# Another layout for the tokens of k and v: five on each of 112 partitions and the last 16 apart, in place of four on each of 128 and separate rest rows

## The chip, the cores and the metric

The kernel runs on one core of a Trainium2 chip. The metric is the device time of one execution in microseconds (us). A run counts as fast or slow by its state, and verdicts use fast runs alone. A ratio is the mean time of one kernel's fast runs over the mean of the other's fast runs of the same rounds, so it is not quite the ratio of the medians quoted beside it. Intervals are 95%.

## The reference, cut to what matters

```python
# batch 8, heads 8, sequence 576, head dimension 64
phi = lambda x: np.where(x > 0, x, np.exp(x) - 1.0) + 1.0
q_p, k_p = phi(q), phi(k)
kv  = np.einsum('bhsd,bhse->bhde', k_p, v)        # summed over the 576 tokens
z   = np.sum(k_p, axis=2)
num = np.einsum('bhsd,bhde->bhse', q_p, kv)
den = np.einsum('bhsd,bhd->bhs', q_p, z)[..., None] + 1e-06
x   = (num / den).transpose(0, 2, 1, 3).reshape(4608, 512)
out = gelu_tanh(x @ w_in) @ w_out                 # 512 -> 2048 -> 512
```

576 tokens are four and a half times 128. The sum over tokens does not depend on their order, so k and v may be laid out over the partitions in any way, as long as both are laid out alike.

## The kernel before

TensorE is kept busy with the feed-forward layers of one batch (a "stage") while the other engines prepare the attention of later batches. Most loads and all transposes by DMA share one queue, issued by SyncE (SP); the rest rows of later batches are issued by GpSimd (POOL). Of each tensor of a batch, 512 tokens are loaded as four tokens on each of 128 partitions. The other 64 tokens, the "rest rows", of two batches share one tile (64 partitions each).

```python
pld  = tile_pool(name="pld", bufs=6)     # staging tiles of all loads
psm  = tile_pool(name="psm", bufs=2)     # transposed rest rows of q, qtr
px   = tile_pool(name="px", bufs=5)      # result tiles
...
def load_main(src, b, name, eng, parts=1):          # P = 128, C = 4, MAIN = 512
    t = pld.tile([P, H, C * D], FP32, name=name, tag="ld")
    ... out=t[:, i*hs:(i+1)*hs, :],
        in_=src[b, i*hs:(i+1)*hs, 0:MAIN, :].rearrange("h (p c) d -> p h (c d)", c=C)

def load_rest_half(src, t, m, s, eng):              # REST = 64
    eng.dma_start(out=t[REST*s : REST*(s+1)],
                  in_=src[2*m + s, :, MAIN:S, :].rearrange("h p d -> p h d"))
...
vps = [const.tile([P, H, C, E], BF16, name=f"vp{i}") for i in range(2)]
vrs = [[const.tile([P, H, E], BF16, name=f"vr{i}{s}") for s in range(2)] for i in range(2)]
...
def kv_mm(b, i, kv_ps, at_i=None):
    for c in range(C):
        nc.tensor.matmul(dst, lhsT=kp[:, c, P*i : P*(i+1)], rhs=vps[b%2][:, 2*i:2*i+2, c, :], ...)
    nc.tensor.matmul(dst, lhsT=kr[:, 0, P*i : P*(i+1)], rhs=vrs[(b//2)%2][b%2][:, 2*i:2*i+2, :], ...)
```

The cuts are marked with "...". The weights w_in and w_out go through the same staging tiles: four pieces each, loaded as f32, cast to bf16 by GpSimd, one half of the last w_out piece by ScalarE.

## Time and profile before

| | before |
|---|---|
| time, median of 3 runs | 296.39 us (295.96 to 296.93) |
| profiled span, granted TensorE clock | 293.6 us, 1.000 |
| TensorE busy / idle in the span | 285.3 / 8.3 us |
| second w_out piece landed (from the trace) | 36.63 us |
| stages 0 to 8 (from one batch's first gelu to the next one's, the last to the end) | 31.8, 30.8, 30.0, 30.1, 30.2, 29.7, 30.2, 27.6, 30.3 us |

The first gelu starts at 22.9 us, and the stages fill the rest. The last stage but one is short because less work lies beside the feed-forward layers there. The prediction below shows the lines of the page and the timeline.

### The profile page before, as it was taken

Reading aid. Unit: us, or ns where it says so; the run is one execution under the profiler, and the core shown is the slowest. Engines: PE = TensorE matmul, PEld = TensorE weight load, DVE = VectorE, ACT = ScalarE, POOL = GpSimd, SP = SyncE. Lnnn points to the kernel's source line nnn. Section 1 sums busy time; section 2 is a strip of 40 time slices with the busy share of each in tenths; the row PEclk is TensorE's granted clock in tenths of the full one; section 3 lists DMA queues with packets and bytes.
Section 4 is the critical chain, followed back from the end, with each engine's and each line's share of the span. In section 5 each row is a group of like instructions: output and inputs, shape, how many; then the busy total and the mean of one; then the engine's idle time right before and its main releaser. Section 6 shows DMA issues by size and latency. Waiting matters only on the chain.

```text
span 293.6 us, 4284 instructions
## 1 busy us (share of the span) xinstructions
PE 285.3 (97%) x1701; PEld 149.8 (51%) x1730; DVE 114.4 (39%) x189; ACT 159.2 (54%) x221; POOL 37.1 (13%) x56
## 2 busy tenths in 40 slices
PE   8999999999999999999999999999999999999995
PEld 6885446644565545544454445544554444444443
DVE  3660576245486684356125652543241000000002
ACT  4657963679955772567255935682560176017400
POOL 8057077400005200000000000000000000000000
PEclk9999999999999999999999999999999999999999
DMA  7999999994599969949913895304241110021032
GB/s 238 328 405 394 370 363 384 318 363 143 151 345 243 185 203 341 190 59 288 307 65 71 245 312 126 71 2 139 75 62 30 71 74 0 4 94 47 0 71 71
DMA packets 63731, 53.23 MB, mean 181 GB/s; under 512 B 31712, under 2 KB 56544, under 8 KB 63712
## 3 DMA queue, kind: packets, MB, share of 16 engines
q1 hardware_dynamic: 60288, 41.82, 50.7%
q10 hardware_dynamic: 2464, 8.52, 7.4%
q0 software_dynamic: 960, 2.62, 3.4%
q8 instruction: 13, 0.21, 0.3%
q14 instruction: 6, 0.05, 0.1%
HBM read 36.70 MB, written 9.44 MB: 157 GB/s over the span
## 4 chain that ended last, share of the span: by engine, by line
PE 84%; DMA 11%; DVE 2%; POOL 1%; issue 1%; SPq 0%; ACT 0%; DVEq 0%
PE o_ps L734 39%; PE h_ps L306 37%; DMA w_st<-in_moe_w_out_dram 8%; DMA q_x<-in_q_dram 3%; PE n_ps L258 3%; PE kv_ps L224 2%; PE o_ps L703 1%; POOL w_out_sb L153 1%; PE t_ps L281 1%; DVE kvbd L247 1%; PE kv_ps L231 1%; SPq L67 0%; ACT q_e L165 0%; PE t_ps L252 0%; DVE xt L388 0%
## 5 line engine op out<-in xcount | busy, mean ns | idle before, releaser
L734 PE MATMUL o_ps<-w_out_sb,g 128*128 128x512 bf16 x547 | 123.7, 379 | 1.3 <-POOL w_out_sb L153 0.4
L306 PE MATMUL h_ps<-xt,w_in_sb 128*128 128x512 bf16 (+2 forms) x566 | 118.9, 353 | 0.8
L691 ACT ACTIVATE g<-h_ps 128x512 bf16<-128x512 f32 x144 | 84.4, 598 | 49.9 <-PE h_ps L306 49.0
L734 PEld LDWEIGHTS <-g 128*128 128x128 bf16 x560 | 54.1, 98 | 63.5 <-issue 1.1
L306 PEld LDWEIGHTS <-w_in_sb 128*128 128x128 bf16 x644 | 58.2, 98 | 54.4 <-issue 0.5
L749 ACT COPY o_sb<-o_ps 128x512 f32<-128x512 f32 x18 | 10.5, 585 | 57.7 <-PE o_ps L734 53.1
L747 DVE COPY o_sb<-o_ps 128x512 f32<-128x512 f32 x17 | 11.7, 689 | 64.5 <-PE o_ps L734 57.2
L270 DVE TENSOR_TENSOR x<-n_ps,r 128x512 bf16<-128x512 f32 x36 | 24.9, 692 | 1.2
L247 DVE CAST kvbd<-kv_ps 64x260 bf16<-64x260 f32 (+1 forms) x16 | 6.5, 409 | 39.2 <-PE kv_ps L231 39.1
L165 ACT ACTIVATE q_e<-q_x 128x2048 bf16<-128x2048 f32 (+1 forms) x10 | 15.5, 1557 | 3.1 <-DMA q_x<-in_q_dram 3.1
L165 ACT ACTIVATE k_e<-k_x 128x2048 bf16<-128x2048 f32 (+1 forms) x9 | 15.5, 1719 | 2.8 <-DMA k_x<-in_k_dram 2.7
L268 DVE RECIPROCAL r<-n_ps 128x8 f32<-128x8 f32 x36 | 7.4, 206 | 24.0 <-PE n_ps L258 24.0
L182 DVE TENSOR_TENSOR k_p<-k_p,k_e 128x2048 bf16<-128x2048 bf16 (+1 forms) x9 | 10.7, 1193 | 13.5 <-ACT k_e L165 13.3
L333 PE MATMUL w_ps<-warm 128*128 128x252 bf16 x94 | 14.0, 315 | 1.1 <-DVE warm L124 1.1
L176 DVE TENSOR_SCALAR q_p<-q_x 128x2048 bf16<-128x2048 f32 (+1 forms) x10 | 10.7, 1068 | 8.8 <-DMA q_x<-in_q_dram 8.8
L306 PE MATMUL h_ps<-xt_rest,w_in_sb 128*128 128x512 bf16 x62 | 13.9, 379 | 0.1
L258 PEld LDWEIGHTS <-qt 128*128 128x128 bf16 x128 | 9.7, 98 | 7.9 <-issue 1.0
L208 DVE CAST vp<-v_x 128x2048 bf16<-128x2048 f32 (+1 forms) x9 | 9.4, 1045 | 9.9 <-DMA v_x<-in_v_dram 9.9
L258 PE MATMUL n_ps<-kvbd,qt 128*128 128x130 bf16 x128 | 12.7, 221 | 0.6 <-ACT kvbd L247 0.2
L224 PEld LDWEIGHTS <-k_p 128*128 128x128 bf16 x128 | 9.6, 96 | 6.1 <-DVE vp L208 0.7
L224 PE MATMUL kv_ps<-vp,k_p 128*128 128x130 bf16 x128 | 11.9, 220 | 0.4 <-DVE vp L208 0.4
L333 PEld LDWEIGHTS <-warm 128*128 128x128 bf16 x94 | 10.4, 114 | 3.2 <-DVE warm L124 1.1
(52 smaller groups left out, 141.3 us busy)
## 6 DMA issues: line engine op xcount, KB each, us to landing
out_dram<-o_sb ACTq DMA_DIRECT2D x16, 512.0 KB, 4.9
k_x<-in_k_dram SPq DMA_DIRECT2D x7, 1024.0 KB, 5.9
v_x<-in_v_dram SPq DMA_DIRECT2D x7, 1024.0 KB, 12.4
q_x<-in_q_dram SPq DMA_DIRECT2D x6, 1024.0 KB, 9.0
w_st<-in_moe_w_in_dram SPq DMA_DIRECT2D x4, 1024.0 KB, 10.1
w_st<-in_moe_w_out_dram SPq DMA_DIRECT2D x4, 1024.0 KB, 11.3
q_x<-in_q_dram SPq DMA_DIRECT2D x4, 512.0 KB, 9.9
k_x<-in_k_dram SPq DMA_DIRECT2D x2, 512.0 KB, 4.1
```

What stands on the lines that cost most here:

```text
L165: nc.scalar.activation(e[:, :, hs, :].rearrange("p c h d -> p h c d"), by_chunk(x[:, hs]), AF.Exp)
L176: nc.vector.tensor_scalar(xp[:, :, hs, :].rearrange("p c h d -> p h c d"), by_chunk(x[:, hs]), 1.0, 1.0, op0=ALU.add, op1=ALU.max,)
L182: nc.vector.tensor_tensor(xp[:, :, hs, :], xp[:, :, hs, :], e[:, :, hs, :], op=ALU.min)
L224: nc.tensor.matmul(dst, lhsT=kp[:, c, P * i : P * (i + 1)], rhs=vps[b % 2][:, 2 * i : 2 * i + 2, c, :], start=(c == 0), stop=False,)
L258: nc.tensor.matmul(n_ps[rows, i // 2, 2 * E * (i % 2) : 2 * E * (i % 2) + 2 * E], lhsT=qt_c[:, i, rows], rhs=kvbd[:, i, :], skip_group_che ...
L270: nc.vector.tensor_tensor(x, n_v[:, :, :, 0:D], r[:, :, :, None].to_broadcast([P, 2, 4, D]), op=ALU.mult,)
L306: nc.tensor.matmul(h_ps[:, tok], lhsT=w_in_sb[:, c, P * m : P * (m + 1)], rhs=xt[:, c, tok], start=(c == 0), stop=(c == KM - 1), skip_grou ...
L333: nc.tensor.matmul(w_ps[:, 0:252], lhsT=warm[:, 0:P], rhs=warm)
L691: nc.scalar.activation(gs[j][:, i, :], ps, AF.Gelu_apprx_tanh)
L734: nc.tensor.matmul(o_pss[t], lhsT=g[:, m, P * t : P * (t + 1)], rhs=w_out_sb[:, m, :], start=(m == 0), stop=(m == MM - 1),)
L747: nc.vector.tensor_copy(dst, o_ps)
L749: nc.scalar.copy(dst, o_ps)
```

## The change

The intent is to be rid of the rest rows of k and v: small loads that reach only half of the partitions, with maps and casts of their own. Tokens 0 to 559 now lie five each on 112 partitions. The last 16 lie on the other 16 partitions, in the fifth chunk only. The fifth matmul sums over all 128 partitions, the first four over 112. Two buffer counts are lowered in the same diff.

```diff
+    CK = 5
+    PK = 112
-    psm = ctx.enter_context(tc.tile_pool(name="psm", bufs=2))
-    px = ctx.enter_context(tc.tile_pool(name="px", bufs=5))
+    psm = ctx.enter_context(tc.tile_pool(name="psm", bufs=1))
+    px = ctx.enter_context(tc.tile_pool(name="px", bufs=4))
...
+    def load_kv(src, b, name, parts=1, eng=nc.sync):
+        t = staged(name, LD).rearrange("p (h x) -> p h x", h=H)
         eng.dma_start(
+            out=t[PK:P, :, C * D :], in_=src[b, :, PK * CK : S, :].rearrange("h p d -> p h d")
         )
+        hs = H // parts
+        for i in range(parts):
+            s = slice(i * hs, (i + 1) * hs)
+            nc.sync.dma_start(
+                out=t[0:PK, s],
+                in_=src[b, s, 0 : PK * CK, :].rearrange("h (p c) d -> p h (c d)", c=CK),
+            )
+        return t
...
-    vps = [const.tile([P, H, C, E], BF16, name=f"vp{i}") for i in range(2)]
-    vrs = [
-        [const.tile([P, H, E], BF16, name=f"vr{i}{s}") for s in range(2)]
-        for i in range(2)
-    ]
+    vps = [const.tile([P, H, CK, E], BF16, name=f"vp{i}") for i in range(2)]
...
+    def pieces(n):
+        if n < CK:
+            return ((slice(0, P), slice(0, n)),)
+        return (slice(0, PK), slice(0, C)), (slice(0, P), slice(C, CK))
...
-        for c in range(C):
+        for c in range(CK):
+            r = slice(0, P if c == C else PK)
             nc.tensor.matmul(
                 dst,
-                lhsT=kp[:, c, P * i : P * (i + 1)],
-                rhs=vps[b % 2][:, 2 * i : 2 * i + 2, c, :],
+                lhsT=kp[r, c, P * i : P * (i + 1)],
+                rhs=vps[b % 2][r, 2 * i : 2 * i + 2, c, :],
```

The exponential, the two maps and the cast of v each loop over `pieces`. Rest rows stay for q alone. In batch 0 the small transfers of the last 16 tokens are issued by ScalarE (`eng=nc.scalar`), all others by SyncE.

## The prediction

> **What bounds the kernel now.** I read the busy table first, then the chain that ended last and the groups, to see whether the engines that the change touches set the time.
>
> ```profile
> PE 285.3 (97%) x1701; PEld 149.8 (51%) x1730; DVE 114.4 (39%) x189; ACT 159.2 (54%) x221; POOL 37.1 (13%) x56
> ...
> PE 84%; DMA 11%; DVE 2%; POOL 1%; issue 1%; SPq 0%; ACT 0%; DVEq 0%
> ```
>
> TensorE is busy in 285.3 of 293.6 us, at a granted clock of 1.0 in every slice. It is idle for 8.3 us, and no more than that can be won unless it gets less work. The chain is 84% TensorE and 11% DMA. Where the DMA part lies, the chain in order of time tells:
>
> ```profile
> 14.28 13.33 DMA w_st<-in_moe_w_out_dram
> 27.66 8.97 DMA w_st<-in_moe_w_out_dram
> 36.68 3.02 POOL w_out_sb L153 x2
> 39.75 1.89 PE o_ps L734 x8
> ```
>
> Up to 39.75 us the chain is the queue of loads: the second w_out piece is issued at 27.66, lands at 36.68, and GpSimd casts it for TensorE. From there on it is nearly all TensorE. So two places have to be priced: the head, where batch 0's k, q and v become the first feed-forward input, and the wait for w_out near 37 us. The timeline shows what TensorE waits for in each.
>
> ```profile
> 14.15 1.29 ACT L208 CAST vp<-v_x 128x512 bf16<-128x512 f32 x2
> 14.25 0.41 DVE L208 CAST vp<-v_x 128x512 bf16<-128x512 f32 x1
> 14.72 0.41 PE L224 MATMUL kv_ps<-vp,k_p 128*128 128x130 bf16 x4 [0.44 <-DVE vp L208]
> 14.81 0.43 DVE L208 CAST vp<-v_x 128x512 bf16<-128x512 f32 x1 [0.15 <-DMA v_x<-in_v_dram]
> ...
> 37.77 0.59 PE L734 MATMUL o_ps<-w_out_sb,g 128*128 128x512 bf16 x2 [0.44 <-POOL w_out_sb L153]
> ```
>
> In the head TensorE waits 0.44 us for v's cast (and 0.57 us more until 18 us, by the windows, in the chain of small steps that follows); near 37 us it waits 0.44 us for w_out. The waits are short because about 10.8 us of filler matmuls cover the first loads. Last, the loads themselves, in windows of 1 us (busy time and count of PE, PEld, DVE, ACT, POOL, then clock, DMA share, GB/s):
>
> ```profile
> 4.00:5.00 1.00, 1.00 (x6) 0.73 (x5) 0.50 (x1) 0.50 (x1) 0.94 (x3) 1.00 1.08 383
> 9.00:10.00 1.00, 1.00 (x11) 0.90 (x10) 0.61 (x2) 0.63 (x1) 0.00 (x0) 1.00 1.19 195
> 13.00:14.00 1.00, 1.00 (x15) 0.95 (x14) 0.90 (x4) 0.88 (x3) 0.00 (x0) 1.00 1.05 406
> ```
>
> The engines of the DMA are full in all three, but k moves at 383 GB/s and the weights at 406, while the stretch where the rest rows of k and v drain falls to 195.
>
> [...]
>
> **The change part by part.**
>
> TensorE: nothing. Before, each pair of heads takes four 128-row chunks and one zero-padded rest matmul. After, it takes four of 112 rows and one of 128: again five matmuls of 130 columns, 160 in all (128 + 32 in the groups, 220 and 218 ns).[...]
>
> VectorE and ScalarE: each map or cast becomes two pieces, and the rest's own goes. For two batches, VectorE drops one rest map (0.42), one minimum (0.42) and two v casts (0.42 each), 1.7 us, and gains a 512-element piece for two maps, two minimums and two casts, six times 0.42 = 2.5 us. That is +0.8 us per pair of batches, +3.4 us in all, on an engine busy 39%. ScalarE gains one exponential of 512 elements (0.61) per pair, +2.4 us, at 54%. From 53 us on these lie beside TensorE: no wait of TensorE on either is longer than 0.7 us there, and they are run half a batch ahead. Cost on the path: 0.
>
> The v cast of the head is on the path. Its pieces of 128x512 on VectorE (0.41) and ScalarE (0.62) each get a second one of 128 elements. From 0.69 for 1024 elements and 0.41 for 512 on VectorE, a piece of 128 is about 0.2; from 1.06 and 0.62 on ScalarE, about 0.3. The last pair of heads waits for two ScalarE pieces more, 0.6 us, but TensorE has 0.3 us of other pairs' matmuls in front. So the head gets about 0.25 us longer. k's maps also grow, from five to six instructions before q: VectorE would be done with k near 8.7 us instead of 7.7, just when the first half of q lands (8.57), so that costs about 0.
>
> Loads: per tensor and batch the bytes are the same, 1.18 MB. Before: 1.05 MB at 380 GB/s (2.76 us) and 0.131 MB at 195 (0.67), 3.43 us.[...] From 8 to 12 us only 1084 KB moved, against 1520 at 380 GB/s, a shortfall of 1.15 us for two rest loads, or 0.57 each, where the rate alone explains 0.33. So I take -0.1 to -0.35 us per tensor. Three such tensors (k, v of batch 0, k of batch 1) precede the second w_out piece: it lands 0.3 to 1.0 us sooner. Of the 0.44 us wait near 37 us most goes, and the 0.25 us lost in the head makes TensorE arrive later there, so the two partly cancel.
>
> Buffers: the result tiles go from five to four and the rest's transposed q from two to one. The second transpose of rest q at 119.26 us now must wait until the first one's matmuls have read theirs, near 129.5. The same queue then holds back the four transposes of batch 4's result (122.85 to 129.9 now) to about 131 to 138. Their reader, the first half at 144.57, is still 5 us away, so I count 0.
>
> Sum: head +0.25, w_out -0.45, rest 0: **296.2 us**.
>
> **The rivals.** First, the 112-row loads are slow[...]. For it: the trace has no such shape, and the head is a DMA queue without slack.[...] At 300 GB/s a tensor takes 4.1 us instead of 3.43, which would make w_out 2 us later and the time about 298[...]. Second, the waits at 8 to 12 us were the real brake on q and v, and without them the head starts earlier: then up to 1 us of the waits in 14 to 18 us and the wait at 37 us go, 295.0. Against it: the filler matmuls have a fixed count, and TensorE reaches q's transposes only after them (11.7 us). Third, the held-back transposes do delay something: VectorE waits for a result tile about 4 us near 130 us and is late for batch 5's k and v. Its slack there is about 10 us; if it were used up, TensorE would show one gap of 1 to 4 us near 144 us, 297 to 300.
>
> **Range and chances.** Everything that can be won is under 2 us, so faster by over 2% (5.9 us) is all but excluded. Slower by that much needs the first rival at its worst. The runs of before span 1 us. Range 295.0 to 298.0.
>
> **What would show it.** Right: matmul busy time near 285 us; no trough to 195 GB/s at 9 us; weight loads of 112 rows at 96 ns; the second w_out piece landed before 36.7; the wait near 37 us under 0.44; no gap near 144 us; VectorE busy near 118 us and ScalarE near 161.6. Wrong: 112-row loads far below 380 GB/s, slower weight loads, or a new wait of over 1 us in TensorE's row.

The marked cuts took out what no trace of the kernel before shows, and with it the terms of the load times after the change. The sum is: head +0.25, w_out -0.45, rest 0, 296.2 us. The cut terms came to 0.1 us less per tensor than the 3.43 us of before. With what the shortfall from 8 to 12 us has beyond its rate (0.57 less 0.33) this made 0.1 to 0.35 us per tensor, and for three tensors the 0.3 to 1.0 us behind the -0.45. That a 112-row load isn't slower was the estimate; no trace showed it. The first rival's worst case, 302 us or more, is cut as well.

## The result, and the profile after

| | before | after |
|---|---|---|
| time, median of 4 fast runs | 296.27 us (295.96 to 296.93) | 315.75 us (313.56 to 316.79) |
| ratio | | 1.0645 [1.0582, 1.0707] |
| profiled span, granted clock | 293.6 us, 1.000 | 313.3 us, 0.988 |
| TensorE busy / idle | 285.3 / 8.3 us | 290.6 / 22.7 us |
| second w_out piece landed | 36.63 us | 41.33 us |
| first gelu | 22.9 us | 23.4 us |
| stage 0 | 31.8 us | 40.2 us |
| stage 1 | 30.8 us | 32.9 us |
| stages 2 and 3 | 30.0, 30.1 us | 30.5, 30.9 us |
| stage 4 | 30.2 us | 37.3 us |
| stages 5 to 8 | 29.7, 30.2, 27.6, 30.3 us | 29.7, 30.2, 27.6, 30.5 us |

The kernel became slower by 6.5%. The stages say where: 8.4 us in stage 0, 2.1 in stage 1, 7.1 in stage 4, 0.5 at the head, 1.3 in stages 2 and 3 together, and 0.2 elsewhere. Stages 5 and 6 hold an attention beside the feed-forward layers as stage 4 does, and they take as long as before, so TensorE's own work didn't become dearer. The page of the changed kernel, its busy line and its chain by engine:

```profile
PE 290.6 (93%) x1730; PEld 150.2 (48%) x1730; DVE 112.7 (36%) x198; ACT 161.3 (51%) x227; POOL 24.5 (8%) x35
...
PE 57%; DMA 27%; SPq 6%; DVE 5%; ACT 2%; issue 1%; POOL 0%; DVEq 0%
```

In the chain that ended last, DMA went from 11% to 27% and the issuing queue of SyncE from 0 to 6%, while TensorE fell from 84% to 57%. Of the 19.7 us in the profiled span, 14.4 are idle time of TensorE (22.7 less 8.3). The other 5.3 us are busy time. 3.1 of these are a lower clock, shown below. For the rest, the trace of before has 29 matmul records fewer (1701 against 1730), and the split isn't settled. What TensorE waits for, from the view of waits (sum in us, count, longest):

```profile
PE n_ps L254 <- DMA qt<-q_p: 8.2, 3, 5.4
PE o_ps L708 <- POOL w_out_sb L159: 6.8, 2, 5.5
```

There are two waits, then: for the transposed q (`qt`), in three places, and for w_out, in two. The second releaser is a cast, but the cast was waiting too. The timeline of the changed kernel around 43 us (start, length, engine, what, and in brackets the idle time before and what ended it):

```profile
41.38 2.88 POOL L159 CAST w_out_sb<-w_st 128x1024 bf16<-128x1024 f32 x2 [9.94 <-DMA w_st<-in_moe_w_out_dram]
43.33 3.14 PE L708 MATMUL o_ps<-w_out_sb,g 128*128 128x512 bf16 x7 [5.45 <-POOL w_out_sb L159]
```

GpSimd was idle for 9.94 us until the w_out piece landed, and cast it at once. So the 0.44 us wait of before is now 5.45 us because the load is late. The loads of the same stretch, in windows of 1 us (busy time and count of PE, PEld, DVE, ACT, POOL, then clock, DMA share, GB/s):

```profile
32.00:33.00 1.00, 1.00 (x7) 0.42 (x5) 0.00 (x0) 0.99 (x2) 0.00 (x0) 1.00 1.15 205
38.00:39.00 1.00, 0.00 (x0) 0.00 (x0) 0.13 (x1) 0.13 (x1) 0.00 (x0) 1.00 1.03 354
39.00:40.00 1.00, 0.00 (x0) 0.00 (x0) 1.00 (x1) 1.00 (x1) 0.00 (x0) 1.00 1.06 391
44.00:45.00 1.00, 1.00 (x4) 0.30 (x3) 0.00 (x0) 0.68 (x2) 0.26 (x1) 0.50 1.13 212
```

The DMA engines are full in all four, at 205 and 212 GB/s while a k or a v moves, and at 354 and 391 while a weight does. Before, k moved at 383 and the weights at 406. So the engines take far longer for the same bytes of k and v. The weights, which the change doesn't touch, are a little slower as well: their packets of 2048 bytes take 88 ns in the median where they took 84. The last line also shows a clock of 0.50. The clock records of the trace have it at 0.5 from 42.97 us on, for 3.41 us. TensorE worked in 3.05 us of these, which costs 1.5 us more.

The second place is in stage 4. The queue of SyncE, from the timeline of before and then of after:

```profile
119.26 2.62 SPq L514 DMA_TRANSPOSE qtr<-qr_p  x2
...
132.09 0.53 SPq L67 DMA_DIRECT2D k_x<-in_k_dram  x1
...
140.10 5.24 SPq L465 DMA_TRANSPOSE qt<-q_p  x4
```

```profile
132.05 11.32 SPq L497 DMA_TRANSPOSE qtr<-qr_p  x2
143.47 5.13 SPq L483 DMA_TRANSPOSE xt<-x  x4
...
150.00 0.53 SPq L86 DMA_DIRECT2D k_x<-in_k_dram  x1
...
155.22 13.62 SPq L449 DMA_TRANSPOSE qt<-q_p  x4
```

The two transposes of rest q (`qtr`) now occupy the queue for 11.32 us instead of 2.62, since the second has to wait for the only buffer. All that stands behind them moves back: the loads of batch 6 are issued at 150.00, and the transposes of batch 5's q come after these loads and take 13.62 us beside them. TensorE's row:

```profile
169.48 0.61 PE L254 MATMUL n_ps<-kvbd,qt 128*128 128x130 bf16 x4 [5.35 <-DMA qt<-q_p]
```

It waits 5.35 us, and again the clock is 0.5 for 3.41 us, from 169.26 on, in 3.19 us of which TensorE works: 1.6 us more. The groups of the changed kernel show what the change did to TensorE's own instructions:

```profile
L227 PE MATMUL kv_ps<-vp,k_p 112*128 112x130 bf16 (+1 forms) x160 | 13.7, 221 | 1.3 <-DVE vp L216 1.3
L227 PEld LDWEIGHTS <-k_p 112*128 112x128 bf16 (+1 forms) x160 | 11.2, 97 | 7.6 <-DVE vp L216 1.4
```

160 matmuls at 221 ns (before 220 and 218) and weight loads at 97 ns (96): no cost. Here the prediction held.

**How the stages add up.** Stage 0: wait for w_out 5.45 less 0.44, half clock 1.5, a second wait for w_out of 1.38 at 56 us: 7.9 of the 8.4 us. Stage 1: one wait of 2.28 us for `qt` near 88 us, against 2.1. Stage 4: 5.35 + 1.6 = 6.95 of 7.1.

### The profile page after: what moved, and what is told of

It reads as the page before. It is cut to its first block, busy times and chain, and to the rows that moved or that the text cites. A ratio compares the mean times of both kernels' runs of the same rounds, so it can differ in the third digit from the quotient of the medians.

```text
span 313.3 us, 4314 instructions
## 1 busy us (share of the span) xinstructions
PE 290.6 (93%) x1730; PEld 150.2 (48%) x1730; DVE 112.7 (36%) x198; ACT 161.3 (51%) x227; POOL 24.5 (8%) x35
## 4 chain that ended last, share of the span: by engine, by line
PE 57%; DMA 27%; SPq 6%; DVE 5%; ACT 2%; issue 1%; POOL 0%; DVEq 0%
PE o_ps L708 26%; PE h_ps L302 25%; DMA qt<-q_p 9%; DMA v_x<-in_v_dram 7%; DMA k_x<-in_k_dram 6%; DMA w_st<-in_moe_w_in_dram 5%; SPq L86 3%; PE n_ps L254 2%; SPq L76 1%; DVE k_p L191 1%; PE kv_ps L227 1%; PE o_ps L677 1%; SPq L110 1%; DVE vp L216 1%; DVE q_p L198 1%
## 5 line engine op out<-in xcount | busy, mean ns | idle before, releaser
L708 PE MATMUL o_ps<-w_out_sb,g 128*128 128x512 bf16 x560 | 126.3, 382 | 6.8 <-POOL w_out_sb L159 6.8
L302 PE MATMUL h_ps<-xt,w_in_sb 128*128 128x512 bf16 (+2 forms) x580 | 121.2, 357 | 0.7 <-POOL w_in_sb L152 0.4
L178 ACT ACTIVATE k_e<-k_x 112x2048 bf16<-112x2048 f32 (+3 forms) x18 | 19.7, 1143 | 8.1 <-DMA k_x<-in_k_dram 8.0
L216 DVE CAST vp<-v_x 112x2048 bf16<-112x2048 f32 (+3 forms) x18 | 12.0, 711 | 21.8 <-DMA v_x<-in_v_dram 21.8
L198 DVE TENSOR_TENSOR k_p<-k_p,k_e 112x2048 bf16<-112x2048 bf16 (+3 forms) x18 | 12.7, 747 | 8.4 <-ACT k_e L178 8.4
L191 DVE TENSOR_SCALAR k_p<-k_x 112x2048 bf16<-112x2048 f32 (+3 forms) x18 | 12.7, 747 | 7.2 <-DMA k_x<-in_k_dram 7.2
L227 PE MATMUL kv_ps<-vp,k_p 112*128 112x130 bf16 (+1 forms) x160 | 13.7, 221 | 1.3 <-DVE vp L216 1.3
L227 PEld LDWEIGHTS <-k_p 112*128 112x128 bf16 (+1 forms) x160 | 11.2, 97 | 7.6 <-DVE vp L216 1.4
L326 PE MATMUL w_ps<-warm 128*128 128x252 bf16 x94 | 13.2, 303 | 1.1 <-DVE warm L137 1.1
```

Source lines behind the costliest of these rows:

```text
L178: nc.scalar.activation(e[r, c, hs, :].rearrange("p c h d -> p h c d"), by_chunk(x[r, hs])[:, :, c], AF.Exp,)
L191: nc.vector.tensor_scalar(xp[r, c, hs, :].rearrange("p c h d -> p h c d"), by_chunk(x[r, hs])[:, :, c], 1.0, 1.0, op0=ALU.add, op1=ALU.max,)
L198: nc.vector.tensor_tensor(xp[r, c, hs, :], xp[r, c, hs, :], e[r, c, hs, :], op=ALU.min)
L216: fn(out=vps[b % 2][r, s, c, 0:D], in_=by_chunk(ld["v", b][r, s])[:, :, c],)
L227: nc.tensor.matmul(dst, lhsT=kp[r, c, P * i : P * (i + 1)], rhs=vps[b % 2][r, 2 * i : 2 * i + 2, c, :], start=(c == 0), stop=(c == CK - 1),)
L302: nc.tensor.matmul(h_ps[:, tok], lhsT=w_in_sb[:, c, P * m : P * (m + 1)], rhs=xt[:, c, tok], start=(c == 0), stop=(c == KM - 1), skip_grou ...
```

## The experiments

The theories at the start, by the letters that the expectations use. **P**: loads to 112 partitions are slow. **D**: the rows of 1280 bytes are slow by their size. **B**: the single buffer of `qtr` holds the queue. **C**: the compute side (the pieces, the smaller pool of result tiles) makes buffers free later. P and D both explain slow loads and differ in what cures them; B explains stage 4; C is the rival to all of them.

### First four: one part undone at a time

**a_rows128.** The five chunks stay, but k and v are loaded to 128 partitions with 1024-byte rows, and the 64 rest tokens go to partitions 0 to 63 of the fifth chunk (a matmul over 64 rows).

```diff
-            out=t[PK:P, :, C * D :], in_=src[b, :, PK * CK : S, :]...
+            out=t[0:REST, :, C * D :], in_=src[b, :, MAIN:S, :]...
-                out=t[0:PK, s], in_=src[b, s, 0 : PK * CK, :]... c=CK
+                out=t[:, s, 0 : C * D], in_=src[b, s, 0:MAIN, :]... c=C
-            r = slice(0, P if c == C else PK)
+            r = slice(0, REST if c == C else P)
```

> The changed kernel, but with k and v loaded as 128 rows of four tokens (1024-byte rows) plus the last 64 tokens on partitions 0 to 63 of the fifth chunk; tiles, pieces and buffer counts as in the changed kernel; the result is right. Theory P (the 112-row transfers are slow[...]): the waits at 38 to 43 us and 55 us go, 296 to 301 us. Rival D (rows of 1280 bytes are slow by their size): the same, since the rows are 1024 bytes again. Rival B (the single buffer of the transposed rest q, which holds the load queue near 132 us, is most of the loss): 308 us or more. Rival C (the extra pieces on VectorE and ScalarE cost the time): 312 or more.

Measured: correct, median 310.47 us, ratio 1.0503 [1.0472, 1.0534]. That missed what P expected: the change was far from undone. Second w_out piece at 38.65, stage 0 35.9, stage 4 36.0. So P is not the whole cause of either. The stages 5 and 6, at 30.6 and 31.0 us, were longer than before (29.7 and 30.2), which no theory foresaw. The timelines of this kernel and of after:

```profile
193.75 0.56 PE L227 MATMUL kv_ps<-vp,k_p 128*128 128x130 bf16 x5
194.24 1.90 PE L302 MATMUL h_ps<-xt,w_in_sb 128*128 128x512 bf16 x8
```

```profile
199.22 0.46 PE L227 MATMUL kv_ps<-vp,k_p 112*128 112x130 bf16 x5
199.52 1.89 PE L302 MATMUL h_ps<-xt,w_in_sb 128*128 128x512 bf16 x8
```

Five matmuls of which the last has 64 rows hold TensorE for 0.49 us until the next one starts; with 112 and 128 rows it is 0.30. Four groups per batch make 0.8 us per stage. So this kernel mixes in a cost of its own.

**a_over128.** Every partition reads 1280 bytes, on 128 partitions that overlap, so 11% more bytes and no tail. Its output is wrong, which doesn't matter for the time.

```diff
-                out=t[0:PK, s],
-                in_=src[b, s, 0 : PK * CK, :].rearrange("h (p c) d -> p h (c d)", c=CK),
+                out=t[:, s],
+                in_=bass.AP(tensor=src.tensor, offset=src[b, s, 0:P, :].offset,
+                            ap=[[C * D, P], [S * D, hs], [1, CK * D]]),
```

> The changed kernel, but k and v are loaded as 128 rows of 1280 bytes, row p starting at token 4p (the rows overlap in the source; wrong result on purpose), with no tail transfer. Only the number of rows differs from the changed kernel, and the loads move 11% more bytes. Theory P: [...]loads run at 380 GB/s or more and the time is 296 to 301 us. Rival D (row size): loads stay near 215 to 290 GB/s, 314 us or more. Rival B: 308 or more.

Measured: 305.2 us, ratio 1.0318 [1.0289, 1.0346]. With more bytes than after, it was 10 us faster than after, though slower than P's 296 to 301. So the number of partitions counts, or the tail, which is gone as well (a_pad128_align_psm2 below has a second transfer for each k and v and loses nothing). But stage 0 was still 35.6 us, with a wait of 2.67 us for w_out, so something else slowed the loads too.

**b_112_16.** The kernel before, with only the loads of k and v cut in two: partitions 0 to 111 and 112 to 127, 1024-byte rows.

```diff
+        cuts = (0, P) if src is q else (0, 112, 128)
         for i in range(parts):
-            eng.dma_start(out=t[:, ...], in_=src[..., 0:MAIN, :]...)
+            for r0, r1 in zip(cuts, cuts[1:]):
+                eng.dma_start(out=t[r0:r1, ...], in_=src[..., C * r0 : C * r1, :]...)
```

> The kernel before, with each load of k and v split into one of partitions 0 to 111 and one of 112 to 127, rows of 1024 bytes as before; nothing else changes and the result is right. Theory P: the 112 rows move at some 270 to 290 GB/s or less[...], so a tensor takes 4.5 us or more instead of 2.8; three tensors precede the second w_out piece, which makes the wait near 37 us 4 to 6 us longer: 301 to 310 us. Rival D (row size): 1024-byte rows are fast, 296 to 298 us. Rivals B and C: 296 to 298.

Measured: correct, median 310.59 us (306.3 to 317.77), ratio of the fast runs 1.0393 [1.0347, 1.0439]. Two of four runs were slow, the profiled one too (clock 0.961), so I use no line of it. The ratio alone decides: the same bytes, rows of 1024 bytes, the buffers and the compute of before, and 3.9% slower. P costs by itself; D, B and C can't explain this run. One rival stays in it, the doubled number of transfers. a_align_psm2 against a_pad128_align_psm2, with two transfers for each k and v in both, and the single loads of the probe speak against it.

**a_psm2.** After, with `psm` at two buffers again. The space for it came from using a part of `xt_rest` for the filler matmuls' operand in place of the tile `warm`; without that the program didn't fit.

```diff
-    psm = ctx.enter_context(tc.tile_pool(name="psm", bufs=1))
+    psm = ctx.enter_context(tc.tile_pool(name="psm", bufs=2))
-    warm = const.tile([P, 252], BF16, name="warm")
+    warm = xt_rest[:, 0, 0:252]
```

> The changed kernel with two buffers again for the transposed rest q (room is made by letting the filler matmuls read a tile that is written only later). Theory P: the loads stay slow in the first 75 us, the waits at 38 to 43 and 55 us stay; only the wait of 5.4 us near 165 us shrinks, since the queue is no longer held from 132 to 143 us: 309 to 313 us. Rival B (this buffer is most of the loss): 296 to 304 us. If slow loads alone make the wait near 165 us: 314 to 317.

Measured: correct, 309.54 us, ratio 1.0477 [1.0414, 1.0541], as expected. Stage 4 is 30.2 us, as before the change, while stage 0 stays at 40.0. So B accounts for stage 4 alone.

### A third cause is formed

P and B together left stage 0 open: in a_rows128 and a_over128 loads to 128 partitions were still slow, and so were the weights. From the trace, the 2048-byte packets of the weights took 84 ns (median) before and 88 to 89 after, and the pieces of w_in landed 2.55 us apart before (17.34, 19.89, 22.45, 25.05) and 2.71 after (18.41, 21.12, 23.84, 26.54). Nothing in the diff touches these loads except where their tiles lie. The program's allocation says that the staging tiles started at 70912, 79104, 103680 bytes within a partition before, all multiples of 256, and at 68800, 79040, 109760 after, all 192 bytes above one: the constant tiles ahead of them had shrunk (`vrs` gone, `vps` larger). This is theory **M**: staging tiles that start 192 bytes above a multiple of 256 slow every load. That the address is the cause was a guess at this point; what the packets show is +5 to 6%. "Aligned" means below that the staging tiles start at multiples of 256 bytes, as before the change.

### Second four: alignment, alone and with the rest

**b_mis192.** The kernel before, with one unused tile of 192 bytes ahead of `warm`, and nothing else.

```diff
+    gap = const.tile([P, 96], BF16, name="gap")
+    nc.gpsimd.memset(gap, 0.0)
```

> The kernel before with nothing changed but 192 bytes of padding ahead of the staging tiles, so that every load lands at an address 192 bytes past a multiple of 256, as in the changed kernel. Theory M ([...]2048-byte packets 88 to 89 ns in the changed kernel, 84 in the one before): packets of 2048 bytes 88 to 89 ns, w_in loads 2.7 us apart instead of 2.55, the second w_out piece lands 1.5 to 2.5 us later, a wait of about 2 us near 38 us and after it some 1.6 us at the halved clock: 298.5 to 301 us. Without M: 295 to 297.

Measured: correct, 300.57 us, ratio 1.0148 [1.0115, 1.0182]. The timeline, and the page's line of the loads of w_in (KB each, median us from issue to landing):

```profile
41.64 5.30 PE L736 MATMUL o_ps<-w_out_sb,g 128*128 128x512 bf16 x16 [3.53 <-POOL w_out_sb L155]
```

```profile
w_st<-in_moe_w_in_dram SPq DMA_DIRECT2D x4, 1024.0 KB, 12.0
```

Before, the wait was 0.44 us and that line read 10.1 us. The pieces of w_in landed 2.70 us apart (18.57, 21.27, 23.98, 26.69), the second of w_out at 40.50 instead of 36.63. An unused tile of 192 bytes costs 4.4 us: M costs by itself. (It moves every tile behind it, not the staging tiles alone; that the loads themselves are slower, the packets of w_in and w_out show, at 88 ns as in after.) GpSimd's one extra memset can't be the cause: the cast that TensorE waits for was itself waiting for the load.

**a_align.** After, with a tile of 64 bytes in the same place, so that the staging tiles are aligned again.

```diff
+    gap = const.tile([P, 32], BF16, name="gap")
+    nc.gpsimd.memset(gap, 0.0)
```

> The changed kernel with 64 bytes of padding, so that the staging tiles start at a multiple of 256 bytes again; nothing else. Theory M with P and B: the w_in loads are 2.55 us apart again, the second w_out piece lands some 2 us sooner than in the changed kernel, but the 112-row loads stay slow and the queue stays held: 310 to 314 us, 2 to 4 below the changed kernel. Without M: as the changed kernel, 314 to 317. If M were the whole of it: 296 to 299.

Measured: correct, 307.6 us (305.18 to 309.47), ratio 1.0378 [1.0328, 1.0427]. Sixty-four bytes of padding win some 8 us of the 19.5, more than I expected. Stage 0 fell from 40.2 to 36.9, stage 1 from 32.9 to 30.9, stage 4 to 34.9.

**a_align_psm2.** Both cures: aligned, and two buffers for `qtr`. What is left of the change's cost is P.

> The changed kernel with the staging tiles aligned and two buffers for the transposed rest q: of the three suspects only the 112-row transfers are left. Theory P: a wait of 3 to 5 us near 38 us with 1.6 us of halved clock after it, about 1 us at 55 us and 2 us near 87 us: 303 to 309 us. If the 112-row transfers were slow only because they are misaligned: 295 to 298.

Measured: correct, 301.53 us, ratio 1.0198 [1.0154, 1.0242], just under what was expected. Stage 0 is 36.4, all others are within 0.6 us of before the change. Its view of waits:

```profile
PE o_ps L710 <- POOL w_out_sb L161: 3.6, 2, 3.3
```

From the trace, the second w_out piece landed at 38.37. k of batch 1, tail and main load together, took 4.80 us from the landing before it (31.39 to 36.19), and v 5.43. Up to 65 us the 1280-byte packets took a median of 69 ns, against 89 in after. So misalignment and the 112 rows make each other worse. On 128 partitions and aligned (a_pad128_align_psm2, the next run) the same two tensors took 2.90 and 2.88 us.

**a_pad128_align_psm2.** P, M and B all undone; the five-chunk tiles, the pieces and the four result tiles stay. k and v come to 128 partitions as in a_rows128, but the fifth chunk is zero-padded and its matmul takes 128 rows.

```diff
+        nc.gpsimd.memset(vps[i][REST:P, :, C, :], 0.0)
...
+        if name == "k_p":
+            nc.gpsimd.memset(xp[REST:P, C], 0.0)
...
-            r = slice(0, P if c == C else PK)
+            r = slice(0, P)
```

> The changed kernel with three things undone at once: k and v are loaded as 128 rows plus 64 rest rows (the fifth chunk zero-padded to 128 rows, so that every matmul again spans all rows; a 64-row matmul had cost 0.2 us more for each group in a_rows128), the staging tiles start at a multiple of 256 bytes again (64 bytes of padding), and the transposed rest q has two buffers. The pieces, casts and maps, the five-chunk tiles and four result buffers stay changed. If [...](P), alignment of the destinations (M) and the held queue (B) are all there is: 295 to 298 us. If the pieces on VectorE and ScalarE or the fewer result buffers matter (C): 299 or more.

Measured: correct, 296.4 us (295.84 to 296.86), ratio 1.0008 [0.9977, 1.0039]. All of the loss is gone, so C costs nothing. The second w_out piece landed at 35.38, 1.25 us sooner than before the change, and yet there is no gain: the two waits for w_out here sum to 0.7 us in its view of waits.

```profile
PE o_ps L714 <- POOL w_out_sb L162: 0.7, 2, 0.4
```

### Third four: B alone, D again, and other cuts of the partitions

**a_pad128_align.** As the last, with the single buffer of after: B alone.

> a_pad128_align_psm2 with one buffer for the transposed rest q again: the held queue (B) alone, with fast and aligned loads. If B costs by itself: the queue is held until the first rest q is read near 131 us, the loads of batch 6 and the transposes of q of batch 5 follow late, and TensorE waits some 1 to 3 us for them near 155 us with 1.6 us of halved clock after it: 298 to 301 us. If B costs only on top of slow loads (the prediction's count of 0): 295 to 297.

Measured: correct, 301.59 us, ratio 1.0188 [1.0158, 1.0218]. Its queue of SyncE, then its view of waits:

```profile
121.03 9.96 SPq L503 DMA_TRANSPOSE qtr<-qr_p  x2
...
144.98 9.12 SPq L455 DMA_TRANSPOSE qt<-q_p  x4
```

```profile
PE n_ps L259 <- DMA qt<-q_p: 2.7, 1, 2.7
```

The queue is held for 9.96 us, the loads of batch 6 start at 137.63, the transposes of `qt` run beside them, and TensorE waits 2.71 us at 151.7 to 154.5 and runs at half clock for 3.41 us from 155.41 on, which costs 1.7. Stage 4 is 34.7 us, 4.5 more than before: 2.7 + 1.7 = 4.4. The prediction priced this at 0.

**a_over128_align_psm2.** The overlapping 1280-byte rows on 128 partitions, aligned and with two buffers. Its output is wrong, which doesn't matter for the time.

> The 128 overlapping rows of 1280 bytes (wrong result on purpose, 11% more bytes, no tail) with aligned tiles and two buffers for the transposed rest q; against a_align_psm2 (301.5) only the number of rows differs. Theory P: packets of 1280 bytes at 55 to 57 ns in the median against 66 there, and although more bytes are moved 296 to 300 us. Rival D (the row size): 66 ns or more, 301 or more.

Measured: 296.9 us (296.55 to 297.52), ratio 1.004 [0.9999, 1.0081]. From the trace, its 1280-byte packets took a median of 55 ns, as many bytes per ns as 1024 in the 46 of before (23 and 22). Rows of 1280 bytes are not slow; D falls.

**b_64_64 and b_32_64_32.** The kernel before, with k and v cut at partition 64, or at 32 and 96. I expected loads to 0 to 63 and to 64 to 127 to be slow and the load to 32 to 95 not to be; that was an estimate which no run had shown yet.

```diff
-        cuts = (0, P) if src is q else (0, 112, 128)
+        cuts = (0, P) if src is q else (0, 64, 128)        # b_64_64
+        cuts = (0, P) if src is q else (0, 32, 96, 128)    # b_32_64_32
```

> The kernel before, each load of k and v split into partitions 0 to 63 and 64 to 127 (1024-byte rows, aligned, right result). Theory P: [...]the packets of k and v take about 90 ns in place of 46, a tensor [...]takes 4.8 us instead of 2.8, the second w_out piece lands 4 to 6 us later: 302 to 309 us. If it is the odd number of 112 rows that is slow, or nothing but the number of transfers: 296 to 299.

> The same with three transfers: partitions 0 to 31, 32 to 95 and 96 to 127. Theory P: [...]about 3.7 us a tensor, 298 to 303 us, clearly below b_64_64 although there are more transfers. Rival (splitting costs by the number of transfers): above b_64_64.

Measured: b_64_64 correct, 311.16 us, ratio 1.0499 [1.0451, 1.0548]; b_32_64_32 correct, median 311.27 us, ratio of its fast runs 1.0507 [1.0462, 1.0551], its profiled run slow. Halves of the partitions are slower still, at more than expected: in b_64_64 three tensors after the head took 5.36, 4.91 and 4.43 us. But the two kernels agree, where I had expected the second to be faster. The only trace of b_32_64_32 is slow, so it decides nothing. In it the same three tensors took 4.95, 3.56 and 3.59 us, so the loads may well be faster as expected, but the first gelu starts at 28.1 us instead of 25.1. Why the whole is no faster isn't shown.

### One probe: single loads, one after another

**probe_shapes.** After the last store, loads of one shape each, every one waiting for the one before it; twice each. It has the allocation of a_pad128_align_psm2. Nothing else moves, so a load's duration is its own.

> a_pad128_align_psm2 with a row of single loads after its last store, each of which waits for the one before, so that nothing else is in the queue: k's first rows to 128, 112, 96, 64, 32 or 16 partitions, from different first partitions, in rows of 1024, 1280 and 256 bytes, and at destinations 0, 64 and 192 bytes past a multiple of 256; twice over. The output stays right; only the durations count. Theory P[...]: 8 rows of 1024 bytes to each of 128 partitions in 2.7 us plus a fixed part of about 2 us; 112 partitions take longer than 128 although they are fewer bytes; partitions 0 to 63 and 64 to 127 take 2.4 us plus the fixed part, nearly what 128 partitions take, and partitions 32 to 95 take half of that (1.3 us plus the fixed part); packets at 46 ns in the 128-row load and near 90 in the 64-row loads from 0.[...] Theory M: 128 rows at 192 bytes take 5 to 10% longer than at 0.

Measured: correct; its whole time, 466.6 us, says nothing, and its state is unknown. From the trace:

| destination, 1024-byte rows if not said otherwise | issue to landing, us | packet, ns (mean) |
|---|---|---|
| 128 partitions | 5.09, 5.38, 5.11 (the very first 5.70) | 50 to 53 |
| 0 to 111 | 5.36, 5.61 | 61 to 62 |
| 16 to 127 | 5.26, 5.58 | 56 to 59 |
| 0 to 63 | 4.80, 4.93 | 62 to 66 |
| 64 to 127 | 5.01, 4.86 | 64 to 69 |
| 32 to 95 | 4.17, 3.91 | 53 to 54 |
| 128 partitions, +192 bytes | 5.33, 5.43 | 51 to 55 |
| 128 partitions, +64 bytes | 5.52, 5.65 | 50 to 51 |
| 0 to 111, +192 bytes | 5.99, 6.04 | 67 to 68 |
| 128 partitions, 1280-byte rows | 6.17, 5.79 | 61 to 67 |
| 0 to 111, 1280-byte rows | 6.30, 6.43 | 78 to 80 |

Sixty-four partitions take 4.80 to 5.01 us at either end and 3.91 to 4.17 in the middle. The number of partitions and of bytes is the same, so position decides. The packets of the 64-row loads were expected near 90 ns; at 62 to 69 in the mean (46 in the median) they missed that. 112 partitions need as long as 128, with an eighth less to move. Misaligned by 192 bytes, 128 partitions take 0.1 to 0.3 us more and 112 some 0.5 us: two loads each, but in the direction of the whole kernel, where the two costs together are more than their sum. A single load shows little of the difference, as a part of its time is fixed: 16 partitions, 0.13 MB, took 2.71 and 2.61 us, though their packets all started within 0.73 us. (The "about 2 us" of the expectation fits the small stores of before: 32 KB took 2.0 to 2.1 us from issue to landing.)

### The sum

| kernel | P | M | B | second w_out landed, us | stage 0, us | stage 4, us | ratio |
|---|---|---|---|---|---|---|---|
| before | | | | 36.63 | 31.8 | 30.2 | 1 |
| a_pad128_align_psm2 | | | | 35.38 | 32.1 | 30.2 | 1.0008 |
| b_mis192 | | yes | | 40.50 | 36.4 | 30.2 | 1.0148 |
| a_align_psm2 | yes | | | 38.37 | 36.4 | 30.2 | 1.0198 |
| a_pad128_align | | | yes | 35.10 | 32.1 | 34.7 | 1.0188 |
| a_psm2 | yes | yes | | 41.58 | 40.0 | 30.2 | 1.0477 |
| a_align | yes | | yes | 38.37 | 36.9 | 34.9 | 1.0378 |
| after | yes | yes | yes | 41.33 | 40.2 | 37.3 | 1.0645 |

Alone, M, P and B cost 1.48, 1.98 and 1.88%, 5.3% together, of 6.45%. P with B costs what their sum is (3.78 against 3.86), for they act in different stages. P with M costs 4.77 against 3.46, so about 1.3% is their joint effect: in the trace, packets of 89 ns instead of 69, and the new wait in stage 1 (34.2 us in a_psm2, 30.9 in a_align_psm2). The runs of these kernels were made each against its own runs of before, and the intervals are 0.3 to 0.6% to each side. By the 2% of the verdicts M alone counts as the same, and P and B alone as unclear; all three intervals lie clear of 1. M with B, without P, was not run.

## Why the prediction was wrong

It said 296.2 us in a range of 295.0 to 298.0; the result was 315.75.

- **TensorE's work costs nothing more: right.** 221 ns and 97 ns per instruction, and stages 5 to 8 unchanged. Matmul busy time rose to 290.6 instead of 285, 3.1 us of it by the half clock.
- **Pieces on VectorE and ScalarE cost nothing: right** (a_pad128_align_psm2). ScalarE was busy for 161.3 us where 161.6 was said. VectorE was busy for 112.7 instead of 118: that is 1.7 less than before. Its records overlap in part; summed over all groups they are 118.8 us against 118.3 before, so the increase was 0.5 and not 3.4 us. The rest pieces that go add up to 8.9 us in the groups of before, not to four times 1.7, mostly as the first pair's were cut in halves; and k's minimum of 2048 elements takes 1222 ns where it took 1336.
- **Loads, "-0.1 to -0.35 us per tensor": the first step that failed.** The prediction took main load and tail together to need 0.1 us less than the 3.43 us of before, an estimate that no trace showed. Tail and main load of k of batch 1 took 5.22 us (33.63 to 38.85), 226 GB/s for 1.18 MB, and v's 4.94 (45.86 to 50.80). Before, with the rest rows, they took 4.11 and 2.92, a mean of 3.5 where the prediction had 3.43. So the second w_out piece landed 4.7 us later, where 0.3 to 1.0 us sooner was said. With aligned tiles they took 4.80 and 5.43, so the 112 rows alone keep them far above the 3.43. The rival had the right suspect, "the 112-row loads are slow", but at 300 GB/s and 298 us it was mis-sized as well: P alone made 301.5. How the 16 engines share 112 rows is not in the trace, so why such a load is slow isn't shown.
- **The place of the staging tiles: not in the prediction at all.** It asked what the change removes and adds, not what it moves. It costs 1.48% by itself, nearly all of it in stage 0 (36.4 us instead of 31.8).
- **Buffers, "so I count 0": the second step that failed.** It saw the held-back transposes, to "about 131 to 138", and asked whether their own reader has slack. It does. The prediction didn't ask about what is behind them in the same queue: the loads of batch 6, then the transposes of `qt`, which TensorE reads. B alone is 1.88%, and in after, where the queue is held for longer, stage 4 loses 7.1 us. The third rival was nearly this one, but put the gap at 144 us and its cause at VectorE; the gap is at 164 to 169.5 us, and the releaser is the DMA.
- **A wait costs its length: wrong.** Of after's four waits over 1 us, those of 5.45 and 5.35 us were accompanied by 3.41 us at half clock each and so cost 1.5 and 1.6 us more; those of 1.38 and 2.28 us were not. The 0.44 us wait of before never showed this.
- **The w_out wait as a gain of 0.45: right in direction where the loads are healthy** (35.38 instead of 36.63 us), and worth nothing even then. (The prediction's 36.68 is the start of the cast; the piece landed at 36.63.)
- **The head, +0.25 by the pieces of v's cast: not borne out.** The first gelu starts at 22.9 us before, at 23.4 in after, but at 22.9 in a_align_psm2 and 21.8 in a_pad128_align_psm2, which have the same pieces. b_mis192, without them, starts it at 23.7. So what the head lost fits M better than the pieces.
- **The trough to 195 GB/s near 9 us: read wrongly.** It is gone in after (349 GB/s), as was said. But of the 195 KB that moved in this microsecond before, only 58 KB were rest rows (packets of 256 bytes); 137 KB were q, whose 1024-byte packets took 91 ns there instead of 46. So the 195 GB/s of this microsecond is not the rate of rest rows.

What stays open: which partitions the 16 engines take of a 112-row load, why b_32_64_32 is no faster than b_64_64, and how the 2.2 us of busy time beyond the half clock divides.

No kernel of these beat the one before. With all three costs undone the time is that of before, but undoing P takes back the 112-row layout itself. That layout, with M and B cured, still costs 2% (a_align_psm2).

## What to carry to other kernels

Before a change in shapes is priced, list what it moves: the addresses of all tiles allocated after the ones that shrink or grow, and the order in each queue after an instruction that can now block. Here loads to 112 partitions cost 1.98% and staging tiles 192 bytes above a multiple of 256 cost 1.48%, each alone, so try loads to all 128 partitions and staging tiles at multiples of 256 bytes; a padding tile of 64 bytes won 8 us here. And when a DMA queue is held for lack of a buffer, follow the queue to the last instruction behind it, not only to that instruction's own reader.

## What else the traces show of loads, the clock and TensorE

- Partitions of a load: single loads (probe_shapes) took 61 to 62 ns per 1024-byte packet on 112 partitions and 50 to 53 on 128; in the full queue, all aligned, 1280-byte packets had a median of 69 ns on 112 partitions (a_align_psm2) against 55 on 128 (a_over128_align_psm2). Position counts too: 53 to 54 ns on partitions 32 to 95, 62 to 69 on 0 to 63 and 64 to 127.
- The destination's address: 192 bytes above a multiple of 256, 2048-byte packets took 88 to 89 ns (b_mis192, after) instead of 84 (before), and the whole kernel of b_mis192 took 1.48% longer.
- The clock: waits of 2.25 us (a_rows128), 2.71 us (a_pad128_align) and 1.95 us (a_psm2) were followed by 3.41 us at 0.5, while one of 2.28 us in after was not. Where a trace has two such stretches between its head and its end, their starts are 47.79 us (a_psm2, b_64_64), 119.47 (a_align, a_over128), 122.88 (a_rows128) and 126.29 us (after) apart, 14, 35, 36 and 37 times 3.413. I cut the fast traces into pieces of 3.413 us, counted from the start of such a stretch. Each stretch followed a piece in which TensorE was idle for at least 1.93 us, and none followed one with 1.72 us or less. The end of a piece cut the 2.28 us wait into 1.01 and 1.27. No run tests this by itself.
- TensorE: weight loads of 112 rows took 97 ns, those of 128 took 96. But a group of five matmuls whose last has 64 rows (a_rows128) held TensorE for 0.49 us, against 0.30 with 112 and 128 rows (after). What is paid there, no run shows.
